# Agent attention with a squared-ReLU feed-forward: attention rows transposed in float32 and split into high and low halves from PSUM

## The chip, the cores and the metric

The kernel runs on one core of one Trainium2 chip. The metric is the device time of one execution in microseconds (us), the median of several runs. Engines are named as in the profile: PE is TensorE's matmul, PEld its weight load, DVE is VectorE, ACT is ScalarE, POOL is GpSimd, and SP is SyncE, whose queue issues the DMAs. "L322" is line 322 of the kernel before.

## The reference

Attention through 49 agent rows, then a two-layer feed-forward over the 49,920 resulting rows of 128. B = 4 batches, N = 12480, C = 128:

```python
def sm(a, b):
    s = scale * (a @ b.transpose(0, 2, 1))
    s = s - s.max(-1, keepdims=True)
    e = np.exp(s)
    return e / (e.sum(-1, keepdims=True) + 1e-09)
a2k = sm(agents, k)
agent_v = a2k @ v
q2a = sm(q, agents)
x = (q2a @ agent_v).reshape(B * N, C)
h = x @ w_in            # 128 x 2048
r = np.maximum(h, 0.0)
return ((r * r) @ w_out).astype(np.float32)
```

## The kernel before, in words

**Folding.** The kernel never forms x. For each batch it makes agent_v (128 x 49, in `a2`) and multiplies it by w_in at once (`w_make`, L262), which gives 49 x 2048 weights W. The hidden layer is then h = W^T P, where P holds the normalized query weights q2a, transposed so that the 49 agents are on partitions.

**Precision.** The feed-forward's matmuls run in fp32r, a float32 operand that streams in one pass with fewer significant bits. So every operand is split: a high half (the value cast to fp32r) and a low half (the value minus the high half). A product takes three terms: high by high, low by high and high by low. For the first matmul the halves are stacked on partitions: `p_a` holds P high (49 partitions), P low (49) and the first X = 28 rows of P high again, 126 in all (K); `w_a` holds W high, W high again and 28 rows of W low. The other R = 21 rows of W low times P high go through `w_b` and `p_b`, four products at a time in four row groups of PE (L351). Rows that have to stand on further partitions are copied there by DMA (`q_spread`, L329 and L331; `w_make` step 3, L268 and L272).

**Token groups.** The rows are processed in 52 groups of 960 (`s`), 13 a batch. A group goes through 16 hidden slices of 128 (`i`, one "slot" each): `mm1` (L348, L351; two slices at once), `relu` and `square` on ACT (L355, L359), `high` and `low` on DVE (`gh` L363, `gl` L367), and four slots later `mm2` (L378), three products for each of two column halves, which accumulate the output of the group in two PSUM banks. `store` copies it out (L395, L396).

**The query side of the next group**, in the same slots: `q_scores` (PE, L285), `q_max`, `q_sub` (DVE, L290, L294), `q_exp` (ACT, L297), `q_sum`, `q_inverse` (DVE, L301 to L305), `q_norm` (POOL, L308: the exponentials times the inverse sum, in `es[s]`, 120 partitions x 8 chunks x 49). Then `q_hi` (ACT, L312) casts these to fp32r into the first 49 columns of each chunk of `pp`, `q_lo` (POOL, L315) subtracts and writes the other 49, `q_transpose` (PE, L322) multiplies each chunk's 98 columns by the identity in fp32r, which puts high and low on 98 partitions of two PSUM banks, and `q_copy` (ACT, L325, once a half of the group) moves the 98 partitions into `p_a`. `q_spread` then issues one DMA for the 28 rows of `p_a` and four for `p_b`, on SP's queue.

**The agent side of the next batch** runs beside the current batch's groups: keys in 13 pieces (`k_scores` L154, `k_copy`, `k_pmax`), then their maximum (`k_max`), then values in 13 pieces (`k_sub` on POOL L180, `k_exp`, `k_hi`, `k_lo` on POOL L190, `v_hi`, `v_lo` on DVE L202, `v_acc` on PE L209, `v_sum` on DVE L225), then `a_final` (which transposes in float32 at L233) and `w_make`. The maximum over keys uses a float32 transpose of 120 x 49 too (L170).

**The order** is written out: every step gets a time in slots, and all steps are issued sorted by it. Each engine runs its steps in that order. The feed-forward's steps have fixed times; for attention a planner (`chain`) puts each step into the first slot in which its engine has no other attention step, at least so many slots behind the step that it needs as the table `hop` says (POOL to PE was 3), and in which no more than two attention banks of PSUM are in use (transposes take both):

```python
hop = {"PE": {"PE": 1, "ACT": 0, "DVE": 0}, "ACT": {"PE": 2, "ACT": 1, "DVE": 0, "POOL": 0, "SP": 0},
       "DVE": {"PE": 2, "ACT": 1, "DVE": 1, "POOL": 1, "SP": 0}, "POOL": {"PE": 3, "ACT": 2, "DVE": 2, "POOL": 1}}
```

Before the first group stands a start phase for batch 0, with times written by hand; its last steps are two quarters of `w_make`, whose DMAs the first `mm1` waits for.

Of the kernel before, what the change touches and what calls it, by code (L numbers as in the profile page):

```python
# [17 lines left out]
P = 128  # L18
CH = 120
# [6 lines left out]
def agent_attention_relu2_kernel(ctx: ExitStack, tc: tile.TileContext, qT, kT, v, agT, w_in, w_out, outT):  # L26
# [101 lines left out]
    a2 = cpool.tile([P, A2], F32, name="a2")  # L128
# [98 lines left out]
    def a_final(step):  # L227

        if step == 0:
            nc.vector.tensor_tensor(acc[:, :C], acc[:, :C], acc[:, C + 2:], op=ALU.add)  # L230
        elif step == 1:
            ps = pss["a"] = bank()
            nc.tensor.transpose(ps[:, :A2], acc[:, :C], ident[:A2, :A2])  # L233
            nc.tensor.matmul(ps[:, P:P + A2], acc[:, C:C + 1].to_broadcast([A2, P]), ident[:A2, :A2], start=True, stop=True)
        elif step == 2:
            t = pss.pop("a")[:, :2 * P].rearrange("p (t x) -> p t x", x=P)
            nc.vector.tensor_copy(av, t[:, :, :A])
            nc.vector.scalar_tensor_tensor(out=av[:, 1], in0=t[:, 1, A:A2], scalar=1e-9, in1=av[:, 1], op0=ALU.add, op1=ALU.add)
            nc.vector.tensor_tensor(av[:, 0], t[:, 0, A:A2], av[:, 0], op=ALU.add)
        else:  # L240
            nc.vector.reciprocal(av[:, 1], av[:, 1])
            nc.vector.tensor_tensor(a2.rearrange("p (t a) -> p t a", a=A), av[:, 0:1].to_broadcast([P, 2, A]), av[:, 1:2].to_broadcast([P, 2, A]), op=ALU.mult)
# [5 lines left out]
    X = 28  # L248
    R = A - X
    K = A2 + X  # L250
    assert K <= P and R <= 32
    W = {}
    w_lo = cpool.tile([A, F], F32R, name="w_lo")

    def w_make(b, f, step):
# [4 lines left out]
        if step == 0:  # L260
            pss["w", f] = bank()
            nc.tensor.matmul(pss["w", f][:A2, :], a2, win_sb[:, sl], start=True, stop=True)  # L262
        elif step == 1:
            nc.scalar.copy(wa[:A2, sl], pss["w", f][:A2, :])
        elif step == 2:
            nc.vector.tensor_tensor(w_lo[:, sl], pss.pop(("w", f))[:A, :], wa[:A, sl].bitcast(F32), op=ALU.subtract)
        else:
            nc.sync.dma_start(out=wa[A2:K, sl].bitcast(F32), in_=w_lo[:X, sl].bitcast(F32))  # L268
# [6 lines left out]
    PT, qs, es, mxs, sms, pps = {}, {}, {}, {}, {}, {}  # L275
# [34 lines left out]
    def q_hi(s):  # L310
        pps[s] = wk.tile([CH, G, A2], F32R, name="pp")
        nc.scalar.copy(pps[s][:, :, :A], es[s])  # L312

    def q_lo(s, eng=nc.gpsimd):
        eng.tensor_tensor(out=pps[s][:, :, A:], in0=es.pop(s), in1=pps[s][:, :, :A].bitcast(F32), op=ALU.subtract)  # L315

    def q_transpose(s):
        PT[s] = (wk.tile([P, 2, TT], F32R, name="p_a"), wk.tile([P, TT], F32R, name="p_b"))
        for half in range(2):
            ps = pss["t", s, half] = bank()  # L320
            for c in range(H):
                nc.tensor.matmul(ps[:A2, c * CH:(c + 1) * CH], pps[s][:, half * H + c, :], ident_r[:CH, :CH], start=True, stop=True)  # L322

    def q_copy(s, half):
        nc.scalar.copy(PT[s][0][:A2, half, :], pss.pop(("t", s, half))[:A2, :TT])  # L325

    def q_spread(s):
        pa, pb = PT[s]
        nc.sync.dma_start(out=pa[A2:K].bitcast(F32), in_=pa[:X].bitcast(F32))  # L329
# [78 lines left out]
    def at(t, f, *args):  # L408
# [5 lines left out]
           "DVE": {"PE": 2, "ACT": 1, "DVE": 1, "POOL": 1, "SP": 0}, "POOL": {"PE": 3, "ACT": 2, "DVE": 2, "POOL": 1}}  # L414
# [35 lines left out]
    reads_bank = (k_copy, k_pmax, k_max, v_sum, a_final, w_make, q_max, q_sub, q_copy)  # L450
# [167 lines left out]
```

## Time and profile before

| | |
|---|---|
| median of 3 runs | 2052.86 us (2051.44 to 2054.33) |
| the profiled execution's own time | 2051.45 us |
| its span in the profile | 2049.7 us |
| mean granted TensorE clock | 0.995 |
| start of the first `mm1` | 72.55 us |
| instructions | 30393 |

A row of a group names the line, the engine, the operation, what it writes and reads, the shapes (partitions x elements; for PE the rows and columns of the weights first), the count, and behind the bar the total busy time and the mean of one in ns, then the idle time ahead of it. A row of one line's view gives the shortest, median and longest duration in ns. A timeline row gives the start and the duration in us; of several merged instructions the duration is the whole stretch. [...] A row of waits gives the engine and the tile that waited, for whom, the total in us, how often, and the longest. A matmul in true float32 is recorded as two weight loads and two matmuls, one in fp32r as one of each.

### The profile page before, as it was taken

The numbers are of one execution on the slowest core, as the hardware profiler recorded it, in microseconds if no ns is written. First come the engines' busy times: TensorE is split into PE (matmuls) and PEld (weight loads), VectorE is DVE, ScalarE is ACT, GpSimd is POOL, SyncE is SP. The second block draws the span as 40 slices with busy tenths as digits, with TensorE's granted clock in tenths as the row PEclk, the third lists the DMA queues.
The fourth block names the chain that finished last, engine by engine and source line by source line (L and its number), as shares of the span: only waits on it lengthen the run. The fifth ranks groups of instructions, "written<-read, shape, count | busy, mean of one in ns | idle before, by whom it ended". The sixth has DMA issues, their size and how long they took to land.

```text
span 2049.7 us, 30393 instructions
## 1 busy us (share of the span) xinstructions
PE 2028.1 (99%) x11010; PEld 1584.9 (77%) x11015; DVE 1823.4 (89%) x2274; ACT 1730.2 (84%) x2166; POOL 230.8 (11%) x196
## 2 busy tenths in 40 slices
PE   9899999999999999999999999999999999999999
PEld 8678877777778877777777878777777777777777
DVE  7678899999888889999998888999998888989897
ACT  2488889899888888999888888999888888889897
POOL 0100002221000001232100000122210000000000
PEclk9899999999999999999999999999999999999999
DMA  9322212211121212222112121122111111101010
GB/s 310 90 67 66 71 48 70 79 49 40 56 66 57 66 61 70 61 68 60 35 46 79 56 72 60 61 68 70 45 36 50 44 31 45 30 30 41 29 35 25
DMA packets 51446, 125.16 MB, mean 61 GB/s; under 512 B 7072, under 2 KB 16560, under 8 KB 51296
## 3 DMA queue, kind: packets, MB, share of 16 engines
q1 hardware_dynamic: 51198, 123.19, 19.4%
q8 instruction: 86, 1.41, 0.3%
q14 instruction: 64, 0.52, 0.1%
q10 hardware_dynamic: 98, 0.04, 0.0%
HBM read 81.37 MB, written 25.56 MB: 52 GB/s over the span
## 4 chain that ended last, share of the span: by engine, by line
PE 86%; DVE 8%; issue 4%; DMA 1%; ACT 1%; SPq 0%; ACTq 0%; DVEq 0%
PE out L378 51%; PE h L348 16%; PE h L351 8%; PE ps_att L154 3%; PE ps_att L285 3%; DVE gh L363 3%; DVE gl L367 2%; PE ps_att L322 1%; PE ps_att L209 1%; DVE vs L202 1%; DMA vt<-v 1%; PE ps_att L262 1%; PE h L154 0%; DVE ob L396 0%; PE out L495 0%
## 5 line engine op out<-in xcount | busy, mean ns | idle before, releaser
L367 DVE TENSOR_TENSOR gl<-g,gh 128x960 fp32r<-128x960 f32 x832 | 1015.8, 1221 | 30.6
L355 ACT ACTIVATE r<-h 128x960 f32<-128x960 f32 x832 | 764.4, 974 | 179.0 <-PE h L351 175.8
L359 ACT ACTIVATE g<-r 128x960 f32<-128x960 f32 x832 | 825.5, 1016 | 5.1 <-DVE gl L367 5.1
L378 PE MATMUL out<-gh,wo_hi 128*128 128x480 f32 x1664 | 689.6, 414 | 5.2 <-DVE ob L396 3.6
L363 DVE CAST gh<-g 128x960 fp32r<-128x960 f32 x832 | 583.1, 701 | 99.2 <-ACT g L359 88.0
L378 PE MATMUL out<-gl,wo_hi 128*128 128x480 f32 x1664 | 633.3, 381 | 1.4 <-DVE gl L367 1.1
L378 PE MATMUL out<-gh,wo_lo 128*128 128x480 f32 x1664 | 515.8, 381 | 0.0
L348 PE MATMUL h<-p_a,w_a 126*128 126x480 f32 x1664 | 436.7, 384 | 3.2 <-DMA w_b<-w_lo 2.2
L378 PEld LDWEIGHTS out<-gh,wo_hi 128*128 128x128 f32 x1664 | 313.0, 188 | 141.1 <-issue 71.6
L348 PEld LDWEIGHTS h<-p_a,w_a 126*128 126x128 f32 x1664 | 310.1, 189 | 54.9 <-issue 4.9
L378 PEld LDWEIGHTS out<-gh,wo_lo 128*128 128x128 f32 x1664 | 312.6, 188 | 49.3
L378 PEld LDWEIGHTS out<-gl,wo_hi 128*128 128x128 f32 x1664 | 313.7, 188 | 41.6 <-DVE gl L367 5.7
L351 PE MATMUL h<-p_b,w_b 21*128 21x480 f32 x1664 | 205.4, 479 | 0.7 <-DMA w_b<-w_lo 0.7
L308 POOL TENSOR_TENSOR e<-e,sm 120x392 f32<-120x392 f32 x52 | 55.1, 1060 | 1331.1 <-DVE sm L305 1179.8
L351 PEld LDWEIGHTS h<-p_b,w_b 21*128 21x128 f32 x1664 | 80.2, 182 | 139.9 <-issue 138.1
L285 PEld LDWEIGHTS ps_att<-ag_sb,qt 128*120 128x120 f32 x832 | 96.8, 187 | 3.5
L285 PE MATMUL ps_att<-ag_sb,qt 128*120 128x49 f32 x832 | 94.3, 267 | 0.0
L154 PEld LDWEIGHTS ps_att<-ag_sb,kt 128*120 128x120 f32 x720 | 83.9, 188 | 3.2 <-issue 0.4
L154 PE MATMUL ps_att<-ag_sb,kt 128*120 128x49 f32 x720 | 81.8, 267 | 0.1
L190 POOL TENSOR_TENSOR pe<-sk,pe 120x392 fp32r<-120x392 f32 x39 | 52.9, 1358 | 234.9 <-ACT pe L187 193.0
L158 ACT COPY sk<-ps_att 120x392 f32<-120x392 f32 x45 | 21.9, 487 | 64.8 <-PE ps_att L154 64.8
L315 POOL TENSOR_TENSOR pp<-e,pp 120x392 fp32r<-120x392 f32 x52 | 55.9, 1074 | 161.5 <-ACT pp L312 157.2
(93 smaller groups left out, 936.1 us busy)
## 6 DMA issues: line engine op xcount, KB each, us to landing
vt<-v SPq DMA_DIRECT2D x104, 243.8 KB
kt<-kT SPq DMA_DIRECT2D x52, 480.0 KB
qt<-qT SPq DMA_DIRECT2D x52, 480.0 KB
outT<-ob SPq DMA_DIRECT2D x51, 480.0 KB
p_b<-p_a SPq DMA_DIRECT2D x208, 39.4 KB
p_a<-p_a SPq DMA_DIRECT2D x52, 105.0 KB
raw<-w_in SPq DMA_DIRECT2D x4, 512.0 KB
raw<-w_out SPq DMA_DIRECT2D x4, 512.0 KB
```

Source lines behind the costliest of these rows:

```text
L154: nc.tensor.matmul(ps[:CH, c * A:(c + 1) * A], kt[:, c, :], ag_sb[:, b, :], start=True, stop=True)
L190: eng.tensor_tensor(out=pes[n][:, :, A:], in0=piece(n), in1=pes[n][:, :, :A].bitcast(F32), op=ALU.subtract)
L285: nc.tensor.matmul(ps[:CH, c * A:(c + 1) * A], qt[:, c * CH:(c + 1) * CH], ag_sb[:, s // NS, :], start=True, stop=True)
L308: eng.tensor_tensor(out=es[s], in0=es[s], in1=sms.pop(s).to_broadcast([CH, G, A]), op=ALU.mult)
L315: eng.tensor_tensor(out=pps[s][:, :, A:], in0=es.pop(s), in1=pps[s][:, :, :A].bitcast(F32), op=ALU.subtract)
L348: nc.tensor.matmul(hs[x][:, t, :TT], wa[:K, (x % NF) * P:(x % NF + 1) * P], pa[:K, t, :], start=True, stop=False)
L351: nc.tensor.matmul(hs[i + r // 2][:, r % 2, :TT], wb[rows, i % NF // 2, :], pb[rows], start=False, stop=True)
L355: nc.scalar.activation(rs_[i], hs.pop(i)[:, :, :TT], AF.Relu)
L359: nc.scalar.activation(gs[i], rs_.pop(i), AF.Square)
L363: nc.vector.tensor_copy(ghs[i], gs[i])
L367: nc.vector.tensor_tensor(out=gls[i], in0=gs.pop(i), in1=ghs[i].bitcast(F32), op=ALU.subtract)
L378: nc.tensor.matmul(o[t][:, :TT], w[:, j, :], x[:, t, :], start=st, stop=sp)
```

## The change

The order of split and transpose is swapped. `q_hi` and `q_lo` ahead of the transpose go, and with them the tile `pp`. `q_transpose` now transposes the normalized rows themselves, in float32 (the same call as at L170 and L233), with the 49 columns of a chunk as weights, into partitions 0 to 48 of each bank. From PSUM, `q_hi` (ACT, once a half) casts these into `p_a`'s first 49 partitions, and a new `q_lo` (DVE, once a half) subtracts that high half from the PSUM values and writes the low half to `p_a` from partition 64 on (LO = 64). So `p_a` holds high at 0 to 48, low at 64 to 112, and the repeated high rows in the gaps, 15 at 49 to 63 and 14 at 113 to 126: X = 29 rows, K = 127, and R = 20 rows are left for `p_b` and `w_b`. The weights follow the same places: `a2` gets 128 columns with zeros between (a memset on POOL at the start), L262 multiplies with 113 columns of weights instead of 98, and the extra rows take two DMAs instead of one, both in `w_make` and in `q_spread`. The table's hop from POOL to PE becomes 2, and the planner gets the new chain.

```diff
-    a2 = cpool.tile([P, A2], F32, name="a2")
+    a2 = cpool.tile([P, P], F32, name="a2")
+    nc.gpsimd.memset(a2, 0.0)
...
-    X = 28
-    R = A - X
-    K = A2 + X
+    LO = P // 2
+    R = 20
+    X = A - R
+    X1 = LO - A
+    K = LO + A + X - X1
     assert K <= P and R <= 32
+    extra = ((slice(A, LO), slice(0, X1)), (slice(LO + A, K), slice(X1, X)))
...
-            nc.tensor.matmul(pss["w", f][:A2, :], a2, win_sb[:, sl], start=True, stop=True)
+            nc.tensor.matmul(pss["w", f][:LO + A, :], a2[:, :LO + A], win_sb[:, sl], start=True, stop=True)
         elif step == 1:
-            nc.scalar.copy(wa[:A2, sl], pss["w", f][:A2, :])
+            nc.scalar.copy(wa[:LO + A, sl], pss["w", f][:LO + A, :])
...
-            nc.sync.dma_start(out=wa[A2:K, sl].bitcast(F32), in_=w_lo[:X, sl].bitcast(F32))
+            for to, of in extra:
+                nc.sync.dma_start(out=wa[to, sl].bitcast(F32), in_=w_lo[of, sl].bitcast(F32))
...
-    def q_hi(s):
-        pps[s] = wk.tile([CH, G, A2], F32R, name="pp")
-        nc.scalar.copy(pps[s][:, :, :A], es[s])
-
-    def q_lo(s, eng=nc.gpsimd):
-        eng.tensor_tensor(out=pps[s][:, :, A:], in0=es.pop(s), in1=pps[s][:, :, :A].bitcast(F32), op=ALU.subtract)
-
     def q_transpose(s):
         PT[s] = (wk.tile([P, 2, TT], F32R, name="p_a"), wk.tile([P, TT], F32R, name="p_b"))
+        e = es.pop(s)
         for half in range(2):
             ps = pss["t", s, half] = bank()
             for c in range(H):
-                nc.tensor.matmul(ps[:A2, c * CH:(c + 1) * CH], pps[s][:, half * H + c, :], ident_r[:CH, :CH], start=True, stop=True)
-
-    def q_copy(s, half):
-        nc.scalar.copy(PT[s][0][:A2, half, :], pss.pop(("t", s, half))[:A2, :TT])
+                nc.tensor.transpose(ps[:A, c * CH:(c + 1) * CH], e[:, half * H + c, :], ident[:CH, :CH])
+
+    def q_hi(s, half):
+        nc.scalar.copy(PT[s][0][:A, half, :], pss["t", s, half][:A, :TT])
+
+    def q_lo(s, half):
+        pa = PT[s][0]
+        nc.vector.tensor_tensor(out=pa[LO:LO + A, half, :], in0=pss.pop(("t", s, half))[:A, :TT], in1=pa[:A, half, :].bitcast(F32), op=ALU.subtract)
...
-        nc.sync.dma_start(out=pa[A2:K].bitcast(F32), in_=pa[:X].bitcast(F32))
+        for to, of in extra:
+            nc.sync.dma_start(out=pa[to].bitcast(F32), in_=pa[of].bitcast(F32))
...
-           "DVE": {"PE": 2, "ACT": 1, "DVE": 1, "POOL": 1, "SP": 0}, "POOL": {"PE": 3, "ACT": 2, "DVE": 2, "POOL": 1}}
+           "DVE": {"PE": 2, "ACT": 1, "DVE": 1, "POOL": 1, "SP": 0}, "POOL": {"PE": 2, "ACT": 2, "DVE": 2, "POOL": 1}}
...
-                                ("POOL", q_norm, s), ("ACT", q_hi, s), ("POOL", q_lo, s),
-                                ("PE", q_transpose, s), ("ACT", q_copy, s, 0), ("ACT", q_copy, s, 1)])
+                                ("POOL", q_norm, s), ("PE", q_transpose, s), ("ACT", q_hi, s, 0), ("ACT", q_hi, s, 1), ("DVE", q_lo, s, 0), ("DVE", q_lo, s, 1)])
...
-    for x, f in enumerate((q_exp, q_sum, q_inverse, q_norm, q_hi, q_lo)):
+    for x, f in enumerate((q_exp, q_sum, q_inverse, q_norm)):
         at(t0 + 2 * x + 2.2, f, 0)
     at(t0 + 18, q_transpose, 0)
     for x in range(2):
-        at(t0 + 18.1, q_copy, 0, x)
+        at(t0 + 18.1, q_hi, 0, x)
+        at(t0 + 18.2, q_lo, 0, x)
```

More of the change, by code (lines that the diff above doesn't have):

```diff
@@ L448, in chain @@
         return first, t
-    reads_bank = (k_copy, k_pmax, k_max, v_sum, a_final, w_make, q_max, q_sub, q_copy)
+    reads_bank = (k_copy, k_pmax, k_max, v_sum, a_final, w_make, q_max, q_sub, q_hi, q_lo)
     def plan_tokens(s, base, loaded=False):
         first, end = chain(base, [("PE", q_scores, s), ("DVE", q_max, s), ("DVE", q_sub, s), ("ACT", q_exp, s), ("DVE", q_sum, s), ("DVE", q_inverse, s),
-                                ("POOL", q_norm, s), ("ACT", q_hi, s), ("POOL", q_lo, s),
-                                ("PE", q_transpose, s), ("ACT", q_copy, s, 0), ("ACT", q_copy, s, 1)])
+                                ("POOL", q_norm, s), ("PE", q_transpose, s), ("ACT", q_hi, s, 0), ("ACT", q_hi, s, 1), ("DVE", q_lo, s, 0), ("DVE", q_lo, s, 1)])
         if not loaded:
```

4 lines of the change are left out of this document (2 added, 2 removed).

## The prediction, made before the result was known

> **What bounds the kernel now.** I read the page first, then the stretches of the span, the waits inside them, and last single rows.
>
> ```profile
> PE 2028.1 (99%) x11010; PEld 1584.9 (77%) x11015; DVE 1823.4 (89%) x2274; ACT 1730.2 (84%) x2166; POOL 230.8 (11%) x196
> PE 86%; DVE 8%; issue 4%; DMA 1%; ACT 1%; SPq 0%; ACTq 0%; DVEq 0%
> ```
>
> PE is busy nearly all the time and makes up 86% of the chain that ended last, but DVE has a share in it. Where? The span holds 52 token groups of 16 hidden slices ("slots") each, some 35 to 40 us a group. I take one group of the last batch, where only the query side of attention runs beside the feed-forward, and five groups of an earlier batch, in which the values of the next batch are also summed.
>
> ```profile
> core 0: us, PE busy (x) PEld busy (x) DVE busy (x) ACT busy (x) POOL busy (x), PEclk, DMA share, GB/s
> 314.20:507.50 193.30, 191.07 (x1025) 148.30 (x1025) 189.93 (x230) 176.43 (x234) 44.50 (x33) 1.00 0.20 58
> 1690.50:1725.80 35.30, 35.30 (x186) 27.33 (x185) 31.59 (x38) 31.15 (x38) 2.05 (x2) 1.00 0.11 36
> ```
>
> In the lower row PE is busy to the last 0.01 us and DVE has 3.7 us free: a PE-bound group. In the upper row DVE has only 3.4 us free in five groups, nearly all of it the 0.04 us between its chained `gh` and `gl` (80 of them). Who waits there? The weight loads of the second matmul, for the low halves. First the fourth of these groups (430.2 to 468.6), then the fifth:
>
> ```profile
> PEld out L378 <- DVE gl L367: 1.6, 5, 0.7
> ```
> ```profile
> PEld out L378 <- DVE gl L367: 0.2, 1, 0.2
> ```
>
> So there are two regimes: 40 groups in which what PE does counts, and three such value stretches, in whose first four groups (12 in all) what DVE does counts. In the fifth PE hardly waits, so work added there is absorbed.
>
> **PE: eight transposes a group.** Before, L322 multiplies by the identity in fp32r, with 98 columns of weights; after, it is a float32 transpose with 49. Both stream 120 columns. What does such a group cost today?
>
> ```profile
> 1997.47 0.82 PE L322 MATMUL ps_att<-ident_r,pp 120*98 120x120 f32 x8
> 1998.14 0.43 PE L378 MATMUL out<-gh,wo_hi 128*128 128x480 f32 x1
> 1998.41 0.38 PE L378 MATMUL out<-gl,wo_hi 128*128 128x480 f32 x1
> 1998.63 0.38 PE L378 MATMUL out<-gh,wo_hi 128*128 128x480 f32 x1
> ```
>
> From 1997.47 to 1998.41 is 0.94 us, of which one L378 is 0.22 (the next spacing): 0.72 us for eight, or 0.09 each. L170 and L233 are the same float32 transposes, one record each:
>
> ```profile
> L322 PE MATMUL ps_att<-ident_r,pp x412: 218/249/252, 54.1 to 1998.0; 120*98 120x120 f32 x138
> L170 PE MATMUL ps_att<-ident,m x4: 266/266/276, 32.4 to 1287.2; 120*49 120x120 f32 x4
> L262 PE MATMUL ps_att<-win_sb,a x30: 590/592/1172, 67.7 to 1549.0; 128*98 128x512 f32 x30
> 513.33 0.25 PE L233 MATMUL ps_att<-ident,acc 98*128 98x98 f32 x1
> 513.42 0.38 PE L234 MATMUL ps_att<-ident,acc 98*128 98x98 f32 x2
> ```
>
> L322 with its weights in place takes 218 ns; L170, in exactly the new shape, takes 266. A float32 product streams slower: from 120 columns (266) to 512 (592) is 326 ns over 392 columns, 0.83 ns a column, so L170 lies on the line of float32 matmuls. And the operation behind L233 begins 0.09 us after it, which is 98 columns at 0.83 plus a few ns; L322, with the same fixed part, passes its 120 columns in 218 - (266 - 100) = 52 ns. So I take 120 x 0.83 + 3 = 103 ns for each transpose. The weights of 49 columns no longer matter: they load beneath. Eight make 0.82. The weights of the L378 behind them load only once the last one streams:
>
> ```profile
> 1998.08 0.19 PEld L378 LDWEIGHTS out<-gh,wo_hi 128*128 128x128 f32 x1
> 1998.19 0.19 PEld L378 LDWEIGHTS out<-gl,wo_hi 128*128 128x128 f32 x1
> ```
>
> The second load can begin when the first is in use, 0.11 us later, so the last transpose counts 0.11 instead of 0.10: 0.83 in all. Against 0.72 that is **0.11 us a group more**, 4.5 us over 40 groups. Bounds: 103 ns as above, and 52 + 3 = 55 ns if they stream like fp32r (rival A).
>
> [...]
>
> The wider weights of `w_make` (113 columns) load under a 592 ns matmul. K = 127 rows instead of 126 and 20 instead of 21 change no streamed column: nothing.
>
> **DVE and POOL: the low half moves.** POOL loses L315; DVE gains two subtractions of 480 columns a group, from PSUM.
>
> ```profile
> 353.22 1.80 DVE L367 TENSOR_TENSOR gl<-g,gh 128x960 fp32r<-128x960 f32 x1
> 354.94 1.42 DVE L363 CAST gh<-g 128x960 fp32r<-128x960 f32 x1
> 356.40 1.16 DVE L367 TENSOR_TENSOR gl<-g,gh 128x960 fp32r<-128x960 f32 x1
> 357.48 0.69 DVE L202 TENSOR_TENSOR vs<-vt,vs 120x512 fp32r<-120x512 f32 x1
> 358.08 0.65 DVE L363 CAST gh<-g 128x960 fp32r<-128x960 f32 x1
> 358.77 1.16 DVE L367 TENSOR_TENSOR gl<-g,gh 128x960 fp32r<-128x960 f32 x1
> ```
> ```profile
> L266 DVE TENSOR_TENSOR w_lo<-ps_att,w_a x15: 673/676/683, 69.5 to 1550.8; 49x512 fp32r<-49x512 f32 x15
> ```
> ```profile
> L396 DVE COPY ob<-out 128x480 f32<-128x480 f32 x5 | 3.2, 650 | 0.0
> ```
>
> L266 is the new operation with 512 columns: 676 ns. With 480 it is between 676 x 480 / 512 = 634 ns and the 650 ns of a copy of as many columns from PSUM: 0.645 us. What it takes of DVE's time depends on its neighbours. An independent operation starts 0.08 before the end of the one ahead (356.40 + 1.16 against 357.48), a dependent one 0.04 after it (358.08 + 0.65 against 358.77). So each new one costs 0.565 (overlapped) to 0.765 (waiting for the one ahead, and the one behind it not overlapped). No row shows an output that starts at partition 64, so I take the middle, 0.66.
>
> [...]
>
> Against it stands a relief. Where POOL works, DVE pays: the first L367 above took 1.80 and the first L363 1.42 instead of 1.16 and 0.65. How much for one POOL operation? In 314.2 to 507.5:
>
> ```profile
> L367 DVE TENSOR_TENSOR gl<-g,gh 128x960 fp32r<-128x960 f32 x81 | 104.4, 1289 | 3.0
> L363 DVE CAST gh<-g 128x960 fp32r<-128x960 f32 x81 | 59.7, 737 | 0.0
> L202 DVE TENSOR_TENSOR vs<-vt,vs 120x512 fp32r<-120x512 f32 x24 | 19.5, 812 | 0.0
> ```
>
> Above 1160, 650 and 690 these are 129, 87 and 122 ns too long on average: 10.4 + 7.0 + 2.9 = 20.4 us, for the 33 POOL instructions of the stretch's row: 0.62 each. One of these goes in each group. Net: 2 x 0.66 - 0.62 = **0.70 us a group**, 8.4 us over the 12 groups. Its bounds are 0.51 (overlap) and 1.53 (no overlap, and no relief because another POOL operation falls where L315 was). In the 40 other groups DVE's spare time (3.7 us in the row above) takes it in.
>
> **ACT** loses the 528 ns cast and keeps the two copies, which are as long:
>
> ```profile
> L312 ACT CAST pp<-e 120x392 fp32r<-120x392 f32 x52 | 27.4, 528 | 0.0
> L325 ACT CAST p_a<-ps_att 98x480 fp32r<-98x480 f32 x103 | 57.9, 562 | 0.0
> ```
>
> It is not the bound in either stretch: no gain.
>
> **The order.** By the planner's hops, with norm in slot 5 of a group in both, the transposes move from slot 10 to 7 and the last half from slot 11 (copy) to 9 (subtract). So they come nearer to POOL's norm:
>
> ```profile
> 369.29 1.09 POOL L308 TENSOR_TENSOR e<-e,sm 120x392 f32<-120x392 f32 x1 [13.44 <-DVE sm L305]
> 379.10 0.83 PE L322 MATMUL ps_att<-ident_r,pp 120*98 120x120 f32 x8
> ```
>
> Norm ended 8.7 us ahead of L322 in a value stretch; three slots of 193.3 / 80 = 2.4 us take 7.2 of it, and 1.5 us stay. Without this cover PE would wait with the second matmul queued behind, up to 1 us a group. The subtractions make DVE wait for ACT's high half, with the square's casts (L363) queued behind; ACT is ahead of DVE there. SP issues one copy more a group and holds the loads behind it, but the spread can start two slots earlier (4.8 us): hidden. Without that, the next group's first matmul would come one issue (0.8 us, below) late.
>
> **The start** isn't hidden. SP sends the first weights one after the other, and PE waits for them:
>
> ```profile
> 70.21 0.82 SPq L268 DMA_DIRECT2D w_a<-w_lo  x1
> 71.08 1.68 SPq L272 DMA_DIRECT2D w_b<-w_lo  x2
> ```
> ```profile
> 72.55 0.67 PE L348 MATMUL h<-p_a,w_a 126*128 126x480 f32 x2 [2.20 <-DMA w_b<-w_lo]
> ```
>
> L268 becomes two issues, so what is behind it starts 0.8 us later: **0.8 us** (0 to 1.6, as PE also waits for others). The memset of `a2` is at POOL's idle start.
>
> **The sum.** 4.5 + 8.4 + 0.8 = 13.7 us. The profiled execution took 2051.45 us (span 2049.7); it becomes 2065.2. The median of the three runs, 2052.86, is 1.41 above it: 2066.6 us, 0.67% slower. Some 0.2% (4.1 us) is what a measurement here can tell from no change.
>
> **The rivals.** A, *not slower*: the transposes stream at the pace of fp32r. Eight are then 7 x 0.055 + 0.11 for the next weights = 0.50 us, 0.22 less than now. It decides as soon as a transpose takes under some 70 ns. 40 x -0.22 + 8.4 + 0.8 = +0.4: 2053.3, no difference. For it: one record, not two as in L234. Against: 266 ns, and the spacing behind L233. If DVE's work is hidden too: 52 x -0.22 + 0.8 = -10.6, 2042.3, faster (A').
>
> B, DVE is not the bound: its backlog (four slots deep) swallows the net 0.70. Then 52 x 0.11 + 0.8 = 6.5: 2059.4. For it: PE itself is busy 191.07 of 193.30. Against: it waits for `gl` there.
>
> C, DVE's stretches grow: the relief fails to come, or lasts six groups a batch instead of four. 18 x 0.91 (upper end of the step, relief kept) + 34 x 0.11 + 0.8 = 20.9: 2073.8; without relief, 18 x 1.53 + 3.7 + 0.8 = 32.0: 2084.9. For it: no row of an output at partition 64.
>
> That the transposes would split into two records, as a float32 product does, is excluded by L170's four records for four batches.
>
> **How the numbers follow.** Forecast 0.55 (with its own bounds, 0.51 and 0.91 a group and 0 to 1.6 at the start, 2063.5 to 2069.9), B 0.13, C 0.12, A 0.12, A' 0.08. Faster is A' alone, 0.08; same is A, 0.12; slower the rest, 0.80. The range leaves out A' and C's upper half: 2053 to 2078.
>
> **What would show it.** Right: transposes 103 ns apart; two subtractions of about 0.645 us; a plain group (35.2 us) longer by 0.11; the five groups of 193.3 us longer by about 3; DVE without idle time in them and more waiting for `gl`; POOL's L315 gone and fewer L367 of 1.80; the first L348 0.8 later. Wrong: transposes under 70 ns apart, or value stretches that grow no more than plain groups.

## The result and the profile after

| | before | after |
|---|---|---|
| median | 2052.61 us (2051.44 to 2054.33, 4 runs) | 2078.9 us (2078.02 to 2080.93, 4 runs) |
| the profiled execution's own time | 2051.45 us | 2078.28 us |
| its span | 2049.7 us | 2076.5 us |
| mean granted TensorE clock | 0.995 | 0.991 |

The changed kernel is slower: ratio 1.0131, 95% interval 1.0115 to 1.0147. The forecast was 2066.6 us and its range ended at 2078. The sign was right; of the 26.8 us between the two profiled executions the sum held 13.7.

The page of the changed kernel, the two rows that answer to the first fence of the prediction:

```profile
PE 2040.1 (98%) x11015; PEld 1594.9 (77%) x11015; DVE 1854.2 (89%) x2378; ACT 1712.4 (82%) x2114; POOL 174.9 (8%) x145
PE 81%; DVE 10%; issue 6%; ACT 2%; DMA 1%; SPq 0%; ACTq 0%; DVEq 0%
```

POOL lost its 52 subtractions, DVE has 104 more instructions, and the chain moved from PE towards DVE and "issue". That says in which direction, not where. For the place I cut both spans at the first `mm1` of each group (the first start of L348 before, L353 after) and added up the pieces:

| part of the span, us | predicted change | before | after | weights first (below) |
|---|---|---|---|---|
| up to the first `mm1` | +0.8 | 72.6 | 76.1 (+3.5) | 76.4 |
| group 0 | +0.1 | 48.0 | 59.1 (+11.2) | 41.3 |
| three groups 5, 18, 31, ahead of the value groups | +0.3 | 107.6 | 111.8 (+4.2) | 111.8 |
| fifteen value groups (6 to 10 of each batch) | +8.7 | 579.6 | 587.6 (+7.9) | 587.6 |
| the 32 other groups | +3.5 | 1199.9 | 1200.2 (+0.3) | 1200.2 |
| the last group and the end | +0.1 | 41.9 | 41.7 (-0.2) | 41.7 |

The term that I had worked hardest on, the value groups, is about right. The largest one, group 0, stood in the sum with 0.1 us, as any plain group. Stretches of the changed kernel, in the order of the header: group 0, group 5, the five value groups, and a plain group of the last batch:

```profile
core 0: us, PE busy (x) PEld busy (x) DVE busy (x) ACT busy (x) POOL busy (x), PEclk, DMA share, GB/s
76.10:135.20 59.10, 51.58 (x213) 37.30 (x214) 35.45 (x48) 32.32 (x40) 2.36 (x2) 0.77 0.13 38
293.20:330.40 37.20, 36.95 (x195) 28.42 (x195) 34.07 (x43) 33.00 (x44) 4.90 (x4) 1.00 0.26 75
330.40:526.20 195.80, 190.73 (x1020) 147.98 (x1020) 192.00 (x243) 174.66 (x227) 40.06 (x28) 1.00 0.20 56
1717.20:1752.50 35.30, 35.30 (x186) 27.37 (x185) 32.09 (x40) 30.73 (x37) 1.07 (x1) 1.00 0.12 37
```

The lower two answer to the two rows that the prediction quotes: 195.80 against 193.30, and 35.30 against 35.30 (35.288 against 35.250 as a mean over eleven such groups). The first row is the finding: 59.1 us in which PE was idle for 7.5, at a mean granted clock of 0.77. The same stretch before:

```profile
72.60:120.50 47.90, 46.23 (x212) 34.70 (x213) 34.20 (x46) 33.10 (x42) 3.73 (x3) 0.82 0.16 47
278.40:314.20 35.80, 35.80 (x188) 27.55 (x187) 33.34 (x41) 32.50 (x43) 6.49 (x5) 1.00 0.24 69
```

Who waits in group 0 of the changed kernel? Its timeline of PE, rows of three lines: L267 folds a quarter of the weights, L322 transposes for group 1, and L353 is `mm1`.

```profile
97.87 1.10 PE L322 MATMUL ps_att<-ident,e 120*49 120x120 f32 x8
101.47 1.12 PE L353 MATMUL h<-p_a,w_a 127*128 127x480 f32 x4 [2.50 <-DMA w_a<-w_lo]
...
114.08 1.02 PE L267 MATMUL ps_att<-win_sb,a 128*113 128x512 f32 x2
119.86 1.94 PE L353 MATMUL h<-p_a,w_a 127*128 127x480 f32 x4 [4.77 <-DMA w_a<-w_lo]
```

The fourth quarter of batch 0's folded weights is made at 114.08, right ahead of the slices that need it, and PE stands for 4.77 us until its DMAs have landed; for the third quarter it stands 2.50 us. Before, PE made the fourth quarter at 91.28 and SP sent it from 99.98 on, well ahead of its slices:

```profile
91.28 1.02 PE L262 MATMUL ps_att<-win_sb,a 128*98 128x512 f32 x2
...
99.98 0.84 SPq L268 DMA_DIRECT2D w_a<-w_lo  x1
100.86 3.23 SPq L272 DMA_DIRECT2D w_b<-w_lo  x4
```

Why so late? Nothing in the diff moves this step; the planner does. It lets at most two attention banks of PSUM be in use. Before, the transposes of group 1 held both from slot 10 on, and the fourth quarter, which needs one for slots 5 to 7, fitted ahead of them. After, norm feeds the transposes directly, they start in slot 7, and hold both banks until the second subtraction has read them (slot 9, plus one). The fourth quarter finds slot 7 full and goes to slot 11. I had followed in the prediction that the transposes come three slots earlier, and had looked only at what they themselves wait for.

The stalls cost twice. The granted clock was back at 1.00 ahead of the first one, and is low in the stretches after each:

```profile
94.00:100.00 6.00, 4.89 (x27) 3.49 (x26) 5.83 (x9) 5.91 (x8) 1.09 (x1) 1.00 0.02 5
100.00:106.00 6.00, 4.42 (x10) 2.30 (x11) 4.17 (x6) 1.47 (x2) 0.00 (x0) 0.72 0.09 23
106.00:112.00 6.00, 6.00 (x23) 4.61 (x22) 3.66 (x5) 3.20 (x5) 0.00 (x0) 0.71 0.18 38
...
118.00:124.00 6.00, 4.08 (x9) 2.33 (x10) 0.51 (x1) 1.13 (x2) 0.00 (x0) 0.65 0.27 68
124.00:130.00 6.00, 6.00 (x35) 5.39 (x34) 0.91 (x2) 2.21 (x3) 0.00 (x0) 0.78 0.09 38
```

From the rows of group 0, the 11.2 us are 5.9 of more idle time (59.10 - 51.58 = 7.5, against 47.90 - 46.23 = 1.7) and, by estimate, about 5.0 of more time lost to a low clock (the span times what the mean granted clock lacks of 1: 59.1 x 0.23 = 13.6, against 47.9 x 0.18 = 8.6). Not all of that low clock follows these stalls: from some 2 to 12 us after its start the group runs at 0.50 in both kernels.

### The profile page after: what moved, and what is told of

The parts are those of the page before. It is cut to its first block, busy times and chain, and to the rows that moved or that the text cites. A ratio compares the mean times of both kernels' runs of the same rounds, so it can differ in the third digit from the quotient of the medians.

```text
span 2076.5 us, 30485 instructions
## 1 busy us (share of the span) xinstructions
PE 2040.1 (98%) x11015; PEld 1594.9 (77%) x11015; DVE 1854.2 (89%) x2378; ACT 1712.4 (82%) x2114; POOL 174.9 (8%) x145
## 4 chain that ended last, share of the span: by engine, by line
PE 81%; DVE 10%; issue 6%; ACT 2%; DMA 1%; SPq 0%; ACTq 0%; DVEq 0%
PE out L383 47%; PE h L353 15%; PE h L356 7%; DVE gh L368 4%; PE ps_att L155 4%; PE ps_att L291 3%; DVE gl L372 2%; PE ps_att L322 2%; DVE vs L203 2%; ACT r L360 1%; DMA vt<-v 1%; PE ps_att L210 1%; PE out L216 1%; ACT g L364 1%; PE h L155 1%
## 5 line engine op out<-in xcount | busy, mean ns | idle before, releaser
L372 DVE TENSOR_TENSOR gl<-g,gh 128x960 fp32r<-128x960 f32 x832 | 1008.8, 1212 | 31.3 <-DVE gh L368 0.5
L364 ACT ACTIVATE g<-r 128x960 f32<-128x960 f32 x832 | 820.0, 1011 | 11.2 <-DVE gl L372 10.6
L368 DVE CAST gh<-g 128x960 fp32r<-128x960 f32 x832 | 556.6, 669 | 83.7 <-ACT g L364 72.4
L353 PE MATMUL h<-p_a,w_a 127*128 127x480 f32 x1664 | 444.0, 388 | 10.3 <-DMA w_a<-w_lo 7.3
L353 PEld LDWEIGHTS h<-p_a,w_a 127*128 127x128 f32 x1664 | 307.0, 190 | 60.4 <-issue 14.8
L356 PE MATMUL h<-p_b,w_b 20*128 20x480 f32 x1664 | 208.2, 481 | 0.2
L356 PEld LDWEIGHTS h<-p_b,w_b 20*128 20x128 f32 x1664 | 81.2, 182 | 141.9 <-issue 139.5
L329 DVE TENSOR_TENSOR p_a<-ps_att,p_a 49x480 fp32r<-49x480 f32 x103 | 67.0, 650 | 3.2
```

The source lines that it names most:

```text
L329: nc.vector.tensor_tensor(out=pa[LO:LO + A, half, :], in0=pss.pop(("t", s, half))[:A, :TT], in1=pa[:A, half, :].bitcast(F32), op=ALU.subtract)
L353: nc.tensor.matmul(hs[x][:, t, :TT], wa[:K, (x % NF) * P:(x % NF + 1) * P], pa[:K, t, :], start=True, stop=False)
L356: nc.tensor.matmul(hs[i + r // 2][:, r % 2, :TT], wb[rows, i % NF // 2, :], pb[rows], start=False, stop=True)
L364: nc.scalar.activation(gs[i], rs_.pop(i), AF.Square)
L368: nc.vector.tensor_copy(ghs[i], gs[i])
L372: nc.vector.tensor_tensor(out=gls[i], in0=gs.pop(i), in1=ghs[i].bitcast(F32), op=ALU.subtract)
```

## The experiments

The three kernels named "before" start from the kernel before, the hop of three from the changed one, all others from the changed one with the weights first. Ratios are to runs of the kernel before beside them (medians of 2052.4 to 2054.3 us). The last two columns are of one profiled execution each. The first five value groups ran at a mean granted clock of 0.99, not 1.00, in the profiles of the hop of three, the hop of two, the fp32r transposes and both kernels with values from six, which by the estimate of 0.01 of 195 us makes those entries some 2 us longer.

| kernel | median us | ratio, 95% interval | group 0 | first five value groups |
|---|---|---|---|---|
| before | 2052.6 | 1 | 48.0 | 193.3 |
| after | 2078.9 | 1.0131 [1.0115, 1.0147] | 59.1 | 195.8 |
| weights first | 2060.3 | 1.0037 [1.0024, 1.0049] | 41.3 | 195.9 |
| hop of three | 2068.0 | 1.0081 [1.0068, 1.0094] | 51.2 | 196.7 |
| before, weights first | 2048.8 | 0.9987 [0.9978, 0.9995] | 45.2 | 193.3 |
| before, weights first, hop of two | 2053.1 | 1.0002 [0.9994, 1.0011] | 44.3 | 195.2 |
| before, float32 transposes | 2057.7 | 1.0021 [1.0012, 1.0031] | 47.7 | 193.3 |
| fp32r transposes | 2049.4 | 0.9994 [0.9984, 1.0004] | 40.3 | 196.5 |
| low half twice | 2075.1 | 1.0109 [1.0094, 1.0124] | 40.6 | 199.6 |
| low half at partition 0 | 2060.6 | 1.0043 [1.0028, 1.0057] | 46.6 | 194.7 |
| halves swapped | 2061.8 | 1.0044 [1.0032, 1.0056] | 41.6 | 195.9 |
| store on ACT | 2063.4 | 1.0047 [1.0028, 1.0066] | 40.6 | 195.8 |
| values from six | 2069.3 | 1.0069 [1.0055, 1.0083] | 41.6 | 200.4 |
| values from six, low half at 0 | 2071.1 | 1.0086 [1.0071, 1.0102] | 40.6 | 199.0 |

### Is it the order of the fourth quarter?

**Weights first.** The planner places the two late quarters of batch 0 before group 1's query side:

```diff
-    plan_tokens(1, 1, True)
     for f in range(2, F // 512):
         _, e = chain(4 * f - 7, [("PE", w_make, 0, f, 0), ("ACT", w_make, 0, f, 1), ("DVE", w_make, 0, f, 2)])
         at(e + .9, w_make, 0, f, 3)
+    plan_tokens(1, 1, True)
```

> The changed kernel, with the planner placing the last two quarters of the first batch's folded weights (w_make of batch 0) before the first token group's attention instead of after it, so that the float32 transposes no longer push the fourth quarter from slot 5 to slot 11. My theory: of the 26.3 us lost, some 10 us lie in group 0, where the first hidden slices wait for that quarter's matmuls and DMAs. Then group 0 falls from 59 to 48 to 50 us and the time to 2067 to 2070 us; the value stretches stay as they are (groups 6 to 9 at 38.7 to 40.2 us). Rival, that group 0 is long because the clock drops or the loads land late in this start: 2077 to 2080 us, group 0 unchanged.

2060.3 us, 18.6 less than the changed kernel and better than expected. Group 0 of this kernel:

```profile
76.40:117.70 41.30, 41.30 (x212) 31.47 (x213) 35.32 (x48) 32.18 (x40) 2.45 (x2) 0.88 0.20 55
```

PE is never idle. Against 59.10 us there are 7.5 us of idle time less, and 10.3 us of busy time less for the same work. Most of the latter is, by the estimate above, the clock: a granted clock of 0.88 over 41.3 us loses 5.0 us where the changed kernel lost 13.6, so 8.6 of the 10.3; the other 1.7 stay open. All other parts are as in the changed kernel, to 0.4 us.

**Hop of three.** The changed kernel with one number set back:

```diff
-           "DVE": {"PE": 2, "ACT": 1, "DVE": 1, "POOL": 1, "SP": 0}, "POOL": {"PE": 2, "ACT": 2, "DVE": 2, "POOL": 1}}
+           "DVE": {"PE": 2, "ACT": 1, "DVE": 1, "POOL": 1, "SP": 0}, "POOL": {"PE": 3, "ACT": 2, "DVE": 2, "POOL": 1}}
```

> The changed kernel with one number set back: the planner's hop from POOL to PE is 3 again, so the transposes of group 1 hold both attention banks from slot 8 instead of 7, and the fourth quarter of the folded weights fits into slots 5 to 7 as in the kernel before. Theory (the order of that quarter): group 0 falls from 59.1 to about 48 us, all other groups stay, 2067 to 2069 us. Rival (group 0 is long because each quarter's extra rows take two DMAs instead of one on SP's queue): group 0 stays above 55 us, 2075 or more.

2068.0 us, as the theory had it: the transposes start one slot later, and the fourth quarter is back in slots 5 to 7. Group 0 takes 51.2 us, not 48; the largest wait that is left is that for the third quarter:

```profile
99.51 1.12 PE L353 MATMUL h<-p_a,w_a 127*128 127x480 f32 x4 [2.20 <-DMA w_a<-w_lo]
```

So the rival has a part too: PE goes on 3.1 us after SP began to issue that quarter (96.40), where the kernel before needed at most 2.4 (95.77 to 98.13), and the second issue for the extra rows is some 0.85 us of it. The medians differ by 10.9 us for this one number. In the profile group 0 fell by 7.9; that execution, at 2073.6 us, was the slowest of five, and its fifteen value groups took 6.0 us more than those of the changed kernel, at a granted clock of 0.97 to 0.99. How the 10.9 divide in the other executions is not shown.

**Before, weights first.** The same reordering on the kernel before (its third quarter ahead of group 1's query side; the fourth stays in slots 5 to 7).

> The kernel before, its planner placing the third quarter of batch 0's folded weights ahead of group 1's query side. Theory (group 0 of the kernel before holds a stall of its own of about 6 us, behind the third quarter): group 0 falls from 48.0 to about 41.5, 2045 to 2048 us. Rival (the 41.3 us of group 0 with weights first came from the change's shorter query chain): 2051 to 2054 us.

2048.8 us, 0.9987 of the kernel before [0.9978, 0.9995]: it beats both kernels, by less than expected. Group 0 falls to 45.2, not 41.5 us, and the first `mm1` comes 1.6 us later in that profile. Value groups and plain groups are those of the kernel before to 0.1 us. What is left above 41.3 is by the same estimate mostly clock (a granted 0.81 over 45.2 us loses 8.6 us against 5.0); one execution's group 0 is no exact measure, as the low half at partition 0 will show.

**Before, weights first, hop of two.** Both late quarters ahead, for which the hop from POOL to PE has to be 2.

> The kernel before with both late quarters of batch 0's folded weights placed ahead of group 1's query side, for which its transposes need the planner's hop of 2 from POOL to PE. Theory (group 0 waits for these quarters and, after a wait, for the clock): group 0 at 41 to 45 us instead of 48, value stretches as before: 2045 to 2049 us. Rival (hop 2 brings the transposes or the values' products too close to POOL's last step in the stretches): five value groups above 194.5 us instead of 193.3, 2050 to 2054 us.

2053.1 us, within the rival's range, but not by its path. Group 0 falls to 44.3, and the eighteen groups 5 to 10 of the three batches take 692.5 us instead of 687.3, with no work added. Of these 5.2 us, 2.8 lie in groups 5, 18 and 31 (see the question on group 5), and 1.9 in the first value stretch, where the granted clock was 0.99. The other two, at 1.00, take 193.7 and 193.2 us, against 193.1 and 193.2 before. So the hop of 2 by itself adds 0.5 us at most to an undisturbed value stretch, and the 2.5 to 2.9 us by which each grew in the changed kernel are not the planner's in the main.

### What does PE pay for the transposes?

**Before, float32 transposes.** The kernel before, only the transposes changed, 98 columns of weights as before:

```diff
-                nc.tensor.matmul(ps[:A2, c * CH:(c + 1) * CH], pps[s][:, half * H + c, :], ident_r[:CH, :CH], start=True, stop=True)
+                nc.tensor.transpose(ps[:A2, c * CH:(c + 1) * CH], pps[s][:, half * H + c, :], ident[:CH, :CH])
```

> The kernel before, with the transposes of its 98 columns of high and low rows as float32 transposes instead of fp32r matmuls by the identity; all else as before. One part of the change alone. By the prediction's step (102 ns a transpose instead of 86, and the next weights behind them) 0.11 us a group where PE is the bound: 4 to 6 us, 2056 to 2059 us. Rival, that the float32 transposes account for most of the loss: 2065 us and more. Rival, that they cost nothing: 2053 us.

2057.7 us. Plain groups take 35.363 instead of 35.250, so +0.11, and value groups are unchanged. That is the PE step of the prediction, by itself.

**fp32r transposes.** Weights first, with the rows rounded to fp32r and multiplied by the fp32r identity:

```diff
-        es[s] = wk.tile([CH, G, A], F32, name="e")
+        es[s] = wk.tile([CH, G, A], F32R, name="e")
...
-                nc.tensor.transpose(ps[:A, c * CH:(c + 1) * CH], e[:, half * H + c, :], ident[:CH, :CH])
+                nc.tensor.transpose(ps[:A, c * CH:(c + 1) * CH].bitcast(F32R), e[:, half * H + c, :], ident_r[:CH, :CH])
```

> Weights first, and the transposes multiply by the fp32r identity with 49 columns of weights; the attention rows are rounded to fp32r ahead of them, so their low half is left out of what is computed (the subtraction still runs, on zeros). Theory (the float32 pace of 0.83 ns a column is what the transposes cost PE): they come under 70 ns apart, plain groups fall by about 0.35 us, 40 of them give 14: 2044 to 2048 us. Rival A (49-column weight loads set the pace): about 80 ns apart, 0.15 a group, 2053 to 2056. Rival B (something else hides or replaces the PE time): no change, 2059 to 2062.

2049.4 us, 10.9 less than with weights first. The durations of one transpose, this kernel first and the changed kernel second:

```profile
L322 PE MATMUL ps_att<-ident_r,e x412: 217/219/223, 55.5 to 1986.4; 120*49 120x120 f32 x138
```
```profile
L322 PE MATMUL ps_att<-ident,e x412: 263/266/305, 55.7 to 2018.3; 120*49 120x120 f32 x138
```

The two differ by 47 ns, and so do the spacings from start to start, 57 against 103 ns, which are what a transpose takes of PE: the durations are longer and overlap. Where does that reach the end? This kernel's first and second value stretch and a plain group:

```profile
307.50:504.00 196.50, 190.45 (x1020) 147.64 (x1019) 191.49 (x240) 174.63 (x227) 39.14 (x28) 0.99 0.19 56
811.30:1006.50 195.20, 188.80 (x1020) 146.28 (x1019) 191.43 (x240) 174.87 (x227) 39.52 (x28) 1.00 0.20 56
1688.40:1723.40 35.00, 35.00 (x185) 27.09 (x185) 32.11 (x40) 30.77 (x37) 1.06 (x1) 1.00 0.12 37
```

Plain groups lose 0.35 us, the 32 other groups together 10.9. The first five value groups, with 40 transposes that are each shorter, take 196.5 instead of 195.9 us, but at a clock of 0.99; the second five, at 1.00, take 195.3 instead of 195.8. That is 0.5 of the 1.75 us that 0.35 a group would give: there PE is not the main bound.

### What does DVE pay for the low half?

First, how the subtraction stands among its neighbours. DVE in the changed kernel, and then with the low half at partition 0 (start, duration):

```profile
356.02 1.16 DVE L372 TENSOR_TENSOR gl<-g,gh 128x960 fp32r<-128x960 f32 x1
357.21 0.65 DVE L329 TENSOR_TENSOR p_a<-ps_att,p_a 49x480 fp32r<-49x480 f32 x1
357.89 0.66 DVE L368 CAST gh<-g 128x960 fp32r<-128x960 f32 x1
```
```profile
344.35 1.16 DVE L374 TENSOR_TENSOR gl<-g,gh 128x960 fp32r<-128x960 f32 x1
345.43 0.64 DVE L330 TENSOR_TENSOR p_l<-ps_att,p_a 49x480 fp32r<-49x480 f32 x1
345.99 0.64 DVE L370 CAST gh<-g 128x960 fp32r<-128x960 f32 x1
```

In the upper rows the subtraction starts 0.03 us after the end of the one ahead (356.02 + 1.16 against 357.21) and the one behind again 0.03 after its end; in the lower rows both overlap by 0.08. The median over the 102 subtractions that follow an L372 is 0.032 us in the upper kernel and -0.083 in the lower.

**Low half at partition 0.** The subtraction writes a tile at partition 0, and one more DMA carries it to partition 64:

```diff
-        nc.vector.tensor_tensor(out=pa[LO:LO + A, half, :], in0=pss.pop(("t", s, half))[:A, :TT], in1=pa[:A, half, :].bitcast(F32), op=ALU.subtract)
+        nc.vector.tensor_tensor(out=pls[s][:, half, :], in0=pss.pop(("t", s, half))[:A, :TT], in1=pa[:A, half, :].bitcast(F32), op=ALU.subtract)
...
+        nc.sync.dma_start(out=pa[LO:LO + A].bitcast(F32), in_=pls.pop(s).bitcast(F32))
```

> Weights first, and the subtraction writes its low half to a tile at partition 0, from which one more DMA carries it to partition 64. [...] Rival (the gap belongs to reading PSUM or to waiting for ACT's high half): gaps stay at +0.03, 2059 to 2062 us.

The gaps closed, from +0.03 to -0.08 us on both sides, so the rival fell on its gaps. The five value groups went from 195.9 to 194.7 us, 1.2 of the 2.2 us that ten subtractions save by these gaps (0.11 us on each side). The time did not follow: 2060.6 us. In its profiled execution group 0 took 46.6 us, with PE idle for only 0.13 us but the clock at 0.50 from 82 to 94 us and at 0.68 from there to 100, and the six times lie between 2053.6 and 2064.9, so this median doesn't tell. A gain of some 1.5 us (the eighteen groups 5 to 10: 697.9 against 699.4) is shown by the groups, not by the time; it would be more if the second value stretch (195.9 us) had not run at a clock of 0.99, as the third, at 1.00, also took 194.7.

**Halves swapped.** The same end without a DMA: ACT writes the high half at partition 64, DVE the low half at partition 0:

```diff
-        nc.scalar.copy(PT[s][0][:A, half, :], pss["t", s, half][:A, :TT])
+        nc.scalar.copy(PT[s][0][LO:LO + A, half, :], pss["t", s, half][:A, :TT])
...
-        nc.vector.tensor_tensor(out=pa[LO:LO + A, half, :], in0=pss.pop(("t", s, half))[:A, :TT], in1=pa[:A, half, :].bitcast(F32), op=ALU.subtract)
+        nc.vector.tensor_tensor(out=pa[:A, half, :], in0=pss.pop(("t", s, half))[:A, :TT], in1=pa[LO:LO + A, half, :].bitcast(F32), op=ALU.subtract)
```

> Weights first, and the two halves change places: ACT writes the high half at partition 64, DVE's subtraction writes the low half at partition 0 and reads the high half at 64; no DMA more. [...]

2061.8 us, and both gaps stay at +0.03 us, though the subtraction's output now begins at partition 0:

```profile
337.50 1.16 DVE L372 TENSOR_TENSOR gl<-g,gh 128x960 fp32r<-128x960 f32 x1
338.69 0.65 DVE L329 TENSOR_TENSOR p_a<-ps_att,p_a 49x480 fp32r<-49x480 f32 x1
339.37 0.66 DVE L368 CAST gh<-g 128x960 fp32r<-128x960 f32 x1
```

They are 31 to 32 ns on both sides, like those of the change itself, and the five value groups take 195.9 us as before. So an output at partition 0 was not enough: the gap is +0.03 us with the high half at 0 and the low half at 64, +0.03 the other way round, and -0.08 with both at 0. The runs show it for these three places alone, and not why.

**Low half twice.** Weights first, and every subtraction is done twice:

```diff
+        ps = pss.pop(("t", s, half))[:A, :TT]
+        for _ in range(2):
+            nc.vector.tensor_tensor(out=pa[LO:LO + A, half, :], in0=ps, in1=pa[:A, half, :].bitcast(F32), op=ALU.subtract)
```

> As x1_weights_first, with the new subtraction of q_lo on VectorE executed twice into the same place (same output). My theory, VectorE's time decides in the value stretches: each more subtraction costs some 0.80 us of VectorE there (0.65 and no overlap on either side), 1.6 us a group, over 4 to 6 groups a batch and 3 batches: 19 to 29 us more than x1, 2087 to 2098 us, and the plain groups (35.3 us) hardly longer. Rival, that these stretches are longer because the planner moved the steps (transposes nearer to POOL's norm, value steps two slots earlier): at most 3 us more than x1.

2075.1 us, 14.8 more, below the range of the DVE theory and far above the rival's. The five value groups took 199.6, so 3.7 us more for ten subtractions of 0.68 (0.65 and the gap). What DVE's other operations there took, weights first and then this kernel:

```profile
L372 DVE TENSOR_TENSOR gl<-g,gh 128x960 fp32r<-128x960 f32 x82 | 104.4, 1273 | 3.0
L368 DVE CAST gh<-g 128x960 fp32r<-128x960 f32 x82 | 57.7, 704 | 0.3
L203 DVE TENSOR_TENSOR vs<-vt,vs 120x512 fp32r<-120x512 f32 x22 | 16.6, 755 | 0.0
```
```profile
L374 DVE TENSOR_TENSOR gl<-g,gh 128x960 fp32r<-128x960 f32 x82 | 102.1, 1245 | 3.4 <-DVE gh L370 0.5
L370 DVE CAST gh<-g 128x960 fp32r<-128x960 f32 x81 | 58.8, 726 | 0.3
L203 DVE TENSOR_TENSOR vs<-vt,vs 120x512 fp32r<-120x512 f32 x22 | 15.1, 684 | 0.0
```

Above 1160, 650 and 690 ns these are 15.1 us too long in the first kernel and 13.1 in the second: 2.0 of the 6.8 us came back, as if less of DVE's work fell beside POOL's (busy for 35.4 us instead of 40.2), and one cast (81 instead of 82) fell behind the window.

**Store on ACT.** Relief for DVE: the second half of the output copy goes to ACT.

```diff
-        nc.vector.tensor_copy(ob[:, 1, :], o[1][:, :TT])
+        nc.scalar.copy(ob[:, 1, :], o[1][:, :TT])
```

> As x1_weights_first, with the second half of each group's output copied out of PSUM by ScalarE instead of VectorE, which takes 0.57 us off VectorE a group and puts 0.56 us on ScalarE, as much as the removed cast had taken. My theory (VectorE's time decides in the value stretches): 7 to 10 us faster than x1, 2058 to 2062 us, groups 6 to 9 at 38 to 39.5 us. Rival (planner's order decides there): no change to x1, 2067 to 2070 us. A third way, that ScalarE becomes the bound: slower than x1.

2063.4 us, no gain where 7 to 10 us were expected. DVE lost five copies, but its idle time in the five groups rose from 3.8 to 5.4 us (195.8 less the busy 190.35), and its casts grew from 704 to 728 ns. New in the waits of this stretch:

```profile
PE ps_att L322 <- DVE acc L226: 1.3, 3, 0.5
DVE gh L368 <- ACT g L364: 1.1, 5, 0.3
```

DVE now waits for ACT, which took the copies over, and PE for a bank. ACT, 90% busy in this stretch, has little room for more. By these waits DVE's load is the bound only as long as ACT stays ahead of it; no run tests that by itself.

### Why is group 5 longer?

It grew by 1.4 us where 0.1 was expected. In the changed kernel it holds the batch's first value product (L210, eight matmuls 0.12 us apart), which stood in group 6 before. That is the planner again, and either part of the change is enough for it: with the hop of three the product stands in group 5 too, and so it does in the kernel before with a hop of two.

**Values from six.** The planner puts no value product ahead of group 6:

```diff
-            _, end = chain(max(t1 + 3, t2 + 2), [("PE", v_acc, n), ("DVE", v_sum, n)])
+            _, end = chain(max(t1 + 3, t2 + 2, base + 6 * NF), [("PE", v_acc, n), ("DVE", v_sum, n)])
```

> Weights first, and the planner puts no value product on PE before the sixth group of a batch, where the kernel before had its first one too; in the changed kernel the first of the 13 stands in group 5. Theory (group 5 is bound by PE and pays for that product's eight matmuls, while groups 6 to 10 are bound by DVE and gain nothing from their leaving): group 5 falls from 37.2 to 36.2 us, groups 6 to 10 stay at 195.9, 3 us over three batches: 2057 to 2058 us against 2060.3. Rival (group 5 is long because DVE's or POOL's value steps come earlier, not because of the product): group 5 stays above 37, 2060 to 2062 us.

2069.3 us. The edit did more than it was meant to: the second product went from slot 98 to 107, and by then the tile of values that it reads holds the fourth piece, so the sum over values is changed in this kernel and the next. Groups 5, 6, and 7 to 10:

```profile
275.20:311.40 36.20, 35.96 (x187) 27.36 (x186) 33.15 (x42) 32.82 (x44) 4.91 (x4) 1.00 0.28 77
311.40:357.10 45.70, 41.34 (x218) 31.92 (x217) 42.31 (x52) 37.40 (x49) 9.77 (x7) 0.96 0.18 50
357.10:511.80 154.70, 151.54 (x813) 117.94 (x812) 150.28 (x192) 137.27 (x179) 31.23 (x21) 1.00 0.20 56
```

Group 5 fell by the 0.9 us of the theory, but group 6 grew by 5.4. The time says nothing on the question; group 5 alone does.

**Values from six, low half at partition 0.** Both edits together.

> The same, and the subtraction writes a tile at partition 0 that one more DMA carries to partition 64. Theory (both belong to the value stretch and add up): groups 5 to 10 of a batch at 230.5 to 231.5 us instead of 233.1, 2054 to 2056 us. Rival (what DVE gains in the five value groups is given back to another wait): the five groups stay at 195.5 or more, 2057 to 2060 us.

2071.1 us, for the same reason: group 6 takes 45.2 us. Whether the two add up stays open.

The better witness is the kernel before with a hop of two. Its work is that of the kernel before, and its planner too puts the first value product into group 5:

```profile
276.90:313.80 36.90, 36.90 (x197) 28.63 (x196) 33.95 (x42) 33.57 (x45) 6.70 (x5) 1.00 0.26 76
313.80:508.90 195.10, 191.57 (x1020) 148.86 (x1019) 189.78 (x230) 176.21 (x232) 45.18 (x33) 0.99 0.19 56
817.90:1011.50 193.60, 189.97 (x1020) 147.54 (x1018) 189.66 (x231) 176.24 (x232) 45.94 (x33) 1.00 0.19 57
1320.60:1513.80 193.20, 189.80 (x1020) 147.62 (x1019) 189.35 (x231) 176.20 (x232) 46.95 (x33) 1.00 0.19 57
```

Group 5 takes 36.8 us instead of 35.9, for eight matmuls more; and the five value groups don't get shorter by losing them: 193.6 and 193.2 in the two stretches at a clock of 1.00, against 193.1 and 193.2. So of the 4.2 us in groups 5, 18 and 31, some 2.8 come from where the planner put the product.

## Why the prediction was wrong, step by step

**The order: the step that failed.** I wrote that the transposes move from slot 10 to 7 and asked who is late for them. I didn't ask who else plans around them, so the sum held 0.1 us for group 0, as for any plain group. By the planner's rule of two banks the transposes push the fourth quarter of batch 0's weights from slot 5 to slot 11, and PE waits 4.77 us for that quarter and runs at a granted 0.65 and 0.78 in the two slices from 118 to 130 us. Group 0 became 11.2 us longer, where the whole sum lacked 13.1. With that quarter back in its place (hop of three) 7.9 of the 11.2 are gone; the other 3.2 are in the main the wait for the third quarter (2.20 us) and the clock (0.80 in the group's mean). Without any such wait the group is 17.8 us shorter than in the changed kernel (weights first), so the kernel before lost time there too. The same planner put value products into groups 5, 18 and 31; another 2.8.

**PE's transposes** are 103 ns apart, as forecast; alone they cost 0.11 us a plain group, as forecast (float32 transposes in the kernel before). In the changed kernel, as a mean over eleven plain groups, the pair of slots with the transposes and the pair behind it (slots 6 to 9) take 0.10 us more than their counterparts before (slots 10 to 13), but the six other pairs together 0.06 us less, and the 32 groups together grew by 0.3 us instead of 3.5. What shortens those other pairs stays open. Rival A fell: 266 ns, not 219. The fp32r kernel shows what it would have been worth, 10.9 us.

**DVE's subtraction** takes 0.650 us, as forecast. I took the middle of 0.565 and 0.765 for what it costs; it is the upper end, 0.79 from these rows (0.65, 0.03 twice, and the 0.08 that its neighbours no longer overlap). The gaps are +0.03 us on both sides in the changed kernel and with the halves swapped, and -0.08 where the high half that it reads and the low half that it writes both begin at partition 0.

**The relief** was sized at 0.62 us a group. Before, the three kinds of operations were 20.4 us too long in five groups; after, with 28 POOL instructions instead of 33 and means of 1273, 703 and 752 ns (nearly those of weights first, shown with the low half twice), they are 9.3 + 4.3 + 1.4 = 15.0 too long: 1.08 us less a group. Net 2 x 0.79 - 1.08 = 0.50 a group, 2.5 in five, which is what they grew by (195.8 against 193.3). Two errors cancelled, so that the 2.9 of the forecast came out nearly right is luck. No run takes the relief by itself; this sum is worked out, not shown.

**Who waits there** was wrong. I expected more waiting for `gl`. Its 3.5 us of PEld's waits before are 0.9 now; PE and its loads wait at the ends of the groups instead, for the output copies, 11.2 us against 6.1 before:

```profile
PEld out L383 <- DVE ob L401: 4.0, 5, 0.9
...
PEld out L383 <- ACT ob L400: 3.2, 4, 1.7
PE out L383 <- ACT ob L400: 2.1, 2, 1.4
PE out L383 <- DVE ob L401: 1.9, 4, 0.6
...
PEld out L383 <- DVE gl L372: 0.9, 3, 0.4
```

Behind ACT's copies stands DVE in part: ACT's own waits for DVE (tiles `e` and `gl`) grew from 2.5 to 7.3 us. DVE is still the engine with the least idle time, and a shorter PE gains little there (fp32r transposes), so rival B fell. Rival C, a longer DVE stretch, gave 2073.8 to 2084.9 us and so holds the measured time, but not its reason: it needs at least 16.4 us in the eighteen groups 5 to 10, and they grew by 12.1, of which 2.8 are the moved products.

**The start** holds the 0.8 us of the second DMA issue: from the first L262 to the first `mm1` it was 67.75 to 72.55, 4.80 us, and it is 70.44 to 76.06, 5.62 us:

```profile
70.44 1.11 PE L267 MATMUL ps_att<-win_sb,a 128*113 128x512 f32 x2 [0.53 <-DVE a L243]
...
72.92 1.66 SPq L274 DMA_DIRECT2D w_a<-w_lo  x2
```

The other 2.7 us lie ahead of the folding, between the loads of values and PE's backlog at a low clock (0.54 from 34 to 40 us, where it was 1.00 before); over the profiles of all kernels here the first `mm1` lies between 72.6 and 76.6 us, so this part may be of the execution and not of the change; no run settles it.

## What to carry to other kernels

When a step in a planned order becomes shorter or earlier, recompute the plan for every step that shares a resource with it, and look first where the slack is least, here the first group, whose weights are made while it runs. Cut the span at a mark that both kernels have and add up the pieces before explaining anything: 11 us sat in one group of 52. And an engine's load is no bound by itself: taking 3 us of copies off DVE and giving them to ACT moved nothing.

## What the runs showed of the hardware

- The stalls of PE in group 0 cost more than their length. After 2.50 and 4.77 us of waiting the granted clock was 0.72 and 0.71, and then 0.65 and 0.78, in the slices of 6 us quoted above, where it had been 1.00 ahead of the first wait. Against weights first, 7.5 us of idle time came with an estimated 8.6 us lost at a lower clock, though some of that lies ahead of the stalls.
- The clock right after the first `mm1` differed between two executions of much the same work: with weights first it was 0.66 from 82 to 88 us and 1.00 from there on, with the low half at partition 0 it was 0.50 from 82 to 94 us, 0.68 to 100 and then 1.00, and group 0 was 5.3 us longer with PE busy for 46.47 of its 46.60 us (41.30 of 41.30).
- Transposes of a float32 operand, 120 columns each, followed one another every 103 ns, fp32r products with the same 49 columns of weights every 57 ns, and those with 98 columns of weights every 82 ns on average (86 in most). The last two stream as many columns, so in the kernel before the columns alone did not set the pace.
- Of the 6.8 us added to a DVE that was busy for 192.1 of 195.9 us, part came back: with POOL's work unchanged (28 instructions), the other operations were 2.0 us shorter in the five profiled groups with the doubled subtraction.
